# Router logits of a fused attention, MLP and expert kernel: dot products on VectorE instead of TensorE matmuls

## The chip, the cores and the metric

The program runs on one core of a Trainium2 chip. The metric is the device time of one execution in microseconds (us); each kernel is run several times. The engines of the core work in parallel, each through its own queue in order: TensorE (PE for its matmuls, PEld for its weight loads), VectorE (DVE), ScalarE (ACT), GpSimd (POOL) and SyncE (SP), which here only starts DMAs.

## The reference

Attention with a block mask over 4 batches of 576 tokens gives x (2304 tokens by 512). A dense MLP follows, and then a layer of eight experts, of which each token uses one:

```
x = attention(q, k, v)                          # [2304, 512]
h = x @ w_in                                    # [2304, 2048]
y = (max(h, 0) + alpha * min(h, 0)) @ w_out     # [2304, 512]
logits = y @ w_gate                             # [2304, 8]
e = argmax(logits); gate = softmax(logits)[e]
out = gate * (relu(y @ w1[e]) @ w2[e])
```

The change concerns the line of the logits.

## The kernel before

The 2304 tokens are cut into nine groups of 256 (g from 0 to 8, `GT` = 2 halves of 128 tokens each). A group's MLP is 16 blocks f. `l1` of a block (tile `l`, in PSUM, tag `T` with two buffers) is 12 matmuls 128x256: each product is made of three, from a high and a low part of both operands, so that the full precision is kept. VectorE applies the activation (`prelu`, tile `t`, two instructions), ScalarE makes the high part `gh`, GpSimd or VectorE the low part `gl`. `l2` of a block adds to the two accumulators `acc` (one for each half of the tokens), three matmuls 128x512 for each: two that read `gh`, then one that reads `gl`. The high and low parts of a group's input are `xh` and `xl`, four pieces of each with one buffer, made by ScalarE and VectorE out of the tile `xr`, which SP's queue loads; `xr` has one buffer.

After a group's 16th block the accumulators are copied to `y` (two tiles) and stored, and the group is routed. `turn` transposes `y` on TensorE (tile `rt`), ScalarE copies the transpose to `xt`, `logits` multiplies it with the gate's weights (tile `lg`), and VectorE copies eight columns to `L`. Then `most`, `exp` and `choose` find the expert, `rank` (two small matmuls, tile `rk`) and `place` (eleven VectorE instructions, from the sum `run` to the record `ig`) its place in the expert's list, and two scatters on GpSimd's queue (`info` out of `ig`) write it to memory. All scatters write the same tensor, so one waits until the one before it has landed.

What stands in each engine's queue, and in which order, is fixed when the program is built. Each step is a `Task` with the engine (or engines) it may run on, a cost in ns, what it reads and writes, and a priority. `order` walks through time with these costs and takes next the task that can start first, by the priority among those within 100 ns. The attention of later tokens is planned in the same list, so its blocks stand between those of the MLP in groups 0 to 5: `S` the scores, `P` the exponentials (scaled by `sm` on GpSimd or VectorE in parts), `PT` their transposes, `o` the product with v. Groups 6 to 8 have no attention left. The expert layer runs after the plan. Two costs matter here:

```
pl.add([("POOL", 780), ("DVE", 480)], lo, [t, gh], [gl], -5)
for i in range(GT):
    pl.add(("POOL", 1100), lambda on, i=i: steps.scatter(i), [("ig", g)], [("info", g, i)], pr, (1024, 1))
```

The routing of group g runs while group g+1 is computed.

Of the kernel before, what the change touches and what calls it, by code (L numbers as in the profile page):

```python
# [8 lines left out]
F32 = mybir.dt.float32  # L9
# [10 lines left out]
P = 128  # L20
# [3 lines left out]
NT, DM = B * S, H * D  # L24
FF = 2048
E, F2 = 8, 1024
GT = 2
G = P * GT
# [5 lines left out]
RATE = 300  # L34
FIRST = 12
LAG = 2
SC = 1.0 / float(D) ** 0.5
KC = 512 + P
QK = KC + S
# [183 lines left out]
def cols(n):  # L223

    return max(n / 2.4 + 12, 108)
# [67 lines left out]
class Attention:  # L293
# [24 lines left out]
    def plan(A, pl):  # L318
# [4 lines left out]
        for p, c in A.units():  # L323
            left.append(A.unit(pl, p, c, A.prio(p, c), A.soon(p, c), left))
            if (p < HP or A.soon(p, c)) and len(left) > LAG - 1:
                left.pop(0)()
# [21 lines left out]
    def early(A, pl):  # L348
# [3 lines left out]
        for p in range(2 * HP):  # L352
# [8 lines left out]
            def scale(on, p=p, i=i):  # L361
                y = pl[i][:, p % 2, 0:EARLY]
                nc.scalar.mul(y, y, SC)

# [51 lines left out]
    def unit(A, pl, p, c, pr, soon, left):  # L416
# [44 lines left out]
        fn, keys = scores1 if p < NPLAIN or soon else scores, Ss + [("step", 0)]  # L461
        if len(left) == LAG:
            left.pop(0)(ns, fn, ks, keys, pr)
# [146 lines left out]
class Mlp1:  # L610
# [6 lines left out]
    def plan(A, pl):  # L617
        for g in range(NG):
            A.tokens(pl, g)
            for f in range(16):  # L620
                A.l1(pl, g, f)
                if f:
                    A.l2(pl, g, f - 1)
            A.l2(pl, g, 15)
            if g == 0:
                A.W1.split(pl)
            if g < NG - 1:
                A.fins(pl, g)
                A.route_plan(pl, g)

    def tokens(A, pl, g):

        nc, x = A.nc, ("xr", g)
        if g == 0:
            return
        t0, t1 = g * G, g * G + G
        halves = [("xT", p, z) for p in range(NPAIR) for z, (a, b) in enumerate(Attention.HALVES) if a + p // HP * S < t1 and b + p // HP * S > t0]
        if g > 1:
            pl.buf(x, "xr", (P, 4, G))

            def load(on):
                nc.sync.dma_start(pl[x], A.xT[:, g * G:(g + 1) * G].rearrange("(k p) t -> p k t", p=P))

            pl.add(("SP", 450), load, halves, [x], -10, (524288, 180))
        for k in range(4):
            def take(k=k):
                return pl[x][:, k] if g > 1 else pl["xo", k, 1][:, 0:G]

            def hi(on, k=k, take=take):
                nc.scalar.copy(pl["xh", g, k], take())  # L650

            def lo(on, k=k, take=take):
                nc.vector.tensor_sub(pl["xl", g, k], take(), pl["xh", g, k].bitcast(F32))

            for z in ("xh", "xl"):
                pl.buf((z, g, k), f"{z}{k}", (P, G), F32R)
            x = ("xr", g) if g > 1 else ("xo", k, 1)
            pl.add(("ACT", 400), hi, [x], [("xh", g, k)], -10)
            pl.add(("DVE", 470), lo, [x, ("xh", g, k)], [("xl", g, k)], -10)

    def l1(A, pl, g, f):
        nc, l, t, gh, gl = A.nc, ("l", g, f), ("t", g, f), ("gh", g, f), ("gl", g, f)
        pl.buf(l, "T")
        c = slice(P * (f % 4), P * (f % 4) + P)
        pr = 100000 + 100 * (16 * g + f)
        keys = [("i", f // 4, k) for k in range(4)]
        ws = [n for key in keys for n in A.W1.names(key, g)]

        def prelu(on, out):
            x = pl[l][:, 0:G]  # L670
            nc.vector.tensor_scalar(pl[out], x, 0.0, A.K.al[:, f:f + 1], op0=ALU.min, op1=ALU.mult)  # L671
            nc.vector.scalar_tensor_tensor(pl[out], x, 0.0, pl[out], op0=ALU.max, op1=ALU.add)  # L672

        if g == 0:
            pl.buf(gh, "gh", (P, G))

            def plain(on):
                for k in range(4):
                    nc.tensor.matmul(pl[l][:, 0:G], lhsT=A.W1.w[keys[k]][:, c], rhs=pl["xr", g][:, k], start=k == 0, stop=k == 3)

            pl.add(("PE", 16 * cols(G)), plain, ws + [("xr", g)] + [("x0", k) for k in range(4)], [l, ("l1", g, f)], pr)
            pl.add(("DVE", 930), lambda on: prelu(on, gh), [l, ("al",)], [gh], -5)
            return

        pl.buf(t, "t", (P, G))
        pl.buf(gh, "gh", (P, G), F32R)
        pl.buf(gl, "gl", (P, G), F32R)

        def first(on):
            for k in range(4):  # L690
                (wh, wl), xh, xl = (A.W[keys[k]][:, z] for z in range(2)), pl["xh", g, k], pl["xl", g, k]
                for j, (a, b) in enumerate(((wh, xh), (wh, xl), (wl, xh))):
                    nc.tensor.matmul(pl[l][:, 0:G], lhsT=a[:, c], rhs=b, start=k == 0 and j == 0, stop=k == 3 and j == 2)  # L693

        def hi(on):
            (nc.scalar.copy if on == "ACT" else nc.vector.tensor_copy)(pl[gh], pl[t])  # L696

        def lo(on):
            (nc.gpsimd if on == "POOL" else nc.vector).tensor_sub(pl[gl], pl[t], pl[gh].bitcast(F32))  # L699

        pl.add(("PE", 12 * cols(G)), first, ws + [("l1", g - 1, 15)] + [(z, g, k) for z in ("xh", "xl") for k in range(4)], [l, ("l1", g, f)], pr)
        pl.add(("DVE", 930), lambda on: prelu(on, t), [l, ("al",)], [t], -5)
        pl.add([("ACT", 420), ("DVE", 300)], hi, [t], [gh], -5)
        pl.add([("POOL", 780), ("DVE", 480)], lo, [t, gh], [gl], -5)
# [36 lines left out]
    def route_plan(A, pl, g):  # L741
        st, pr = {}, 60000 + 100 * g
        nc = A.nc
        quick = True
        steps = A.route(g, lambda i: pl["y", g, i], st)
        if quick:
            for i in range(GT):
                ps, xt, lg = ("rt", g, i), ("xt", g, i), ("lg", g, i)
                pl.buf(ps, "T")
                pl.buf(xt, "xt")  # L750
                pl.buf(lg, "T")
                pl.add(("PE", 500), lambda on, i=i, ps=ps: steps.turn(i, pl[ps]), [("y", g, i)], [ps], 0)
                pl.add(("ACT", 600), lambda on, xt=xt, ps=ps: nc.scalar.copy(pl[xt], pl[ps]), [ps], [xt], 0)
                pl.add(("PE", 460), lambda on, i=i, xt=xt, lg=lg: steps.logits(i, pl[xt], pl[lg]), [xt], [lg], 0)
                pl.add(("DVE", 160), lambda on, i=i, lg=lg: steps.take(i, pl[lg]), [lg], [("L", g)], 0)
        else:
            for e in range(E):
                wg = ("wg", g, e)
                pl.buf(wg, "wg")
                pl.add(("SP", 450), lambda on, e=e, wg=wg: nc.sync.dma_start(pl[wg], A.wgT[e:e + 1, :].to_broadcast([P, DM])), [("wgT",)], [wg], pr, (262144, 200))  # L760
                for i in range(GT):
                    pl.add(("DVE", 760), lambda on, i=i, e=e, wg=wg: steps.dot(i, e, pl[wg]), [wg, ("y", g, i)], [("L", g)], pr)
        if quick:
            pr = 0
        pl.add(("DVE", 450), lambda on: steps.most(), [], [("L", g)], pr)
        pl.add(("ACT", 300), lambda on: steps.exp(), [("L", g)], [("ex", g)], pr)
        pl.add(("DVE", 1000), lambda on: steps.choose(), [("L", g), ("ex", g)], [("oh", g)], pr)
        rk = ("rk", g)
        pl.buf(rk, "T")
        pl.add(("PE", 300), lambda on: steps.rank(pl[rk]), [("oh", g)], [rk], 0 if quick else 50000)  # L770
        pl.add(("DVE", 2200), lambda on: steps.place(pl[rk]), [rk, ("ex", g), ("oh", g), ("run", g)], [("ig", g), ("run", g + 1)], pr)
        for i in range(GT):
            pl.add(("POOL", 1100), lambda on, i=i: steps.scatter(i), [("ig", g)], [("info", g, i)], pr, (1024, 1))
# [5 lines left out]
class Route:  # L779
# [21 lines left out]
    def take(A, i, lg):  # L801
        A.nc.vector.tensor_copy(A.L()[:, i], lg[:, 0:E])

    def dot(A, i, e, wg):
        t = A.ml.bp.tile([P, 512], F32, tag="xt", bufs=1, name=f"dot{A.n}_{i}_{e}")
        A.nc.vector.scalar_tensor_tensor(t, A.y(i), 1.0, wg, op0=ALU.mult, op1=ALU.mult, accum_out=A.L()[:, i, e:e + 1])

    def most(A):
# [482 lines left out]
                    remainder(r)  # L1291


def moe_kernel(tc, qk, v, qke, ve, w_in, w_out, alpha, w_gate, w1, w2, out):
    nc = tc.nc
    with ExitStack() as ctx:
        dp = ctx.enter_context(tc.tile_pool(name="dram", bufs=1, space=DRAM))
        xT = dp.tile([DM, NT], F32, name="xT")
        x2 = dp.tile([NT + 1, DM], F32, name="x2")
        wgT = dp.tile([E, DM], F32, name="wgT")  # L1300
        info = dp.tile([E * NT, 2], I32, name="info")
        cp = ctx.enter_context(tc.tile_pool(name="consts", bufs=1))
        wp = ctx.enter_context(tc.tile_pool(name="weights", bufs=32))
# [8 lines left out]
        pl, banks, hold = Plan(), Slots(), {}  # L1312
# [121 lines left out]
        ex.run(hold["base"], todo, od, lambda: od.all(K.run[(NG - 1) % 2][0:1, GT]))  # L1434


_INS = ['qk', 'v', 'qke', 've', 'moe_w_in', 'moe_w_out', 'moe_alpha', 'moe2_w_gate', 'moe2_w1', 'moe2_w2']
_OUTS = [((NT, DM), 'float32')]


# [46 lines left out]
```

## Time and profile before

| | |
|---|---|
| three runs | 950.98, 951.15 and 956.93 us, median 951.15 |
| the profiled execution | 951.48 us, of which the profile's span is 949.7 |
| mean granted TensorE clock | 0.976 of full speed |
| busy: PE, PEld | 892.8 and 763.4 us |
| busy: DVE, ACT, POOL | 499.5, 409.7 and 294.1 us |

Busy times add up over the whole span; which engine sets the pace is read stage by stage. Times in the rows are counted from the span's start.

### The profile page before, as it was taken

Reading aid. Unit: us, or ns where it says so; the run is one execution under the profiler, and the core shown is the slowest. Engines: PE = TensorE matmul, PEld = TensorE weight load, DVE = VectorE, ACT = ScalarE, POOL = GpSimd, SP = SyncE. Lnnn points to the kernel's source line nnn. Section 1 sums busy time; section 2 is a strip of 40 time slices with the busy share of each in tenths; the row PEclk is TensorE's granted clock in tenths of the full one; section 3 lists DMA queues with packets and bytes.
Section 4 is the critical chain, followed back from the end, with each engine's and each line's share of the span. In section 5 each row is a group of like instructions: output and inputs, shape, how many; then the busy total and the mean of one; then the engine's idle time right before and its main releaser. Section 6 shows DMA issues by size and latency. Waiting matters only on the chain. (4 is left out here: it accounts for less than half of the span.)

```text
span 949.7 us, 17897 instructions
## 1 busy us (share of the span) xinstructions
PE 892.8 (94%) x6329; PEld 763.4 (80%) x6329; DVE 499.5 (53%) x1215; ACT 409.7 (43%) x1037; POOL 294.1 (31%) x312
## 2 busy tenths in 40 slices
PE   7999989999999999999999999999889998998884
PEld 6656658888888888888999999979778987988763
DVE  4999896657546555656434353546215211613450
ACT  7777765454455446454312121223215222523451
POOL 1555673323343432443222223241212111111110
PEclk9999999999999999999999999999999998998997
DMA  8981002312302122001001010043526211622551
GB/s 340 362 317 56 23 20 74 75 48 71 75 28 76 48 59 94 28 27 36 31 2 45 1 45 2 23 123 101 170 88 222 68 47 56 198 62 80 169 163 62
DMA packets 46267, 85.80 MB, mean 90 GB/s; under 512 B 12191, under 2 KB 18991, under 8 KB 46128
## 3 DMA queue, kind: packets, MB, share of 16 engines
q1 hardware_dynamic: 35264, 64.20, 20.7%
q0 software_dynamic: 4240, 11.56, 3.8%
q10 hardware_dynamic: 6624, 8.39, 2.5%
q8 instruction: 63, 1.03, 0.5%
q14 instruction: 76, 0.62, 0.2%
HBM read 70.85 MB, written 13.67 MB: 89 GB/s over the span
## 5 line engine op out<-in xcount | busy, mean ns | idle before, releaser
L693 PE MATMUL l<-xh,wi 128*128 128x256 f32 x1024 | 206.0, 287 | 0.0
L693 PEld LDWEIGHTS l<-xh,wi 128*128 128x128 f32 x1024 | 167.0, 191 | 4.2 <-issue 0.5
L721 PE MATMUL acc<-wo,gh 128*128 128x512 f32 x512 | 167.3, 408 | 0.0
L693 PE MATMUL l<-xl,wi 128*128 128x256 f32 x512 | 145.0, 283 | 0.1
L699 POOL TENSOR_TENSOR gl<-t,gh 128x256 fp32r<-128x256 f32 x103 | 78.5, 764 | 193.3 <-ACT gh L696 158.4
L671 DVE TENSOR_SCALAR t<-l,al 128x256 f32<-128x256 f32 x128 | 61.9, 484 | 141.6 <-PE l L693 136.1
L696 ACT CAST gh<-t 128x256 fp32r<-128x256 f32 x124 | 50.4, 406 | 186.1 <-DVE t L672 105.3
L529 POOL TENSOR_SCALAR P<-P,sm 128x256 f32<-128x256 f32 (+4 forms) x66 | 78.4, 1195 | 107.7 <-ACT gh L696 39.8
L721 PE MATMUL acc<-wo,gl 128*128 128x512 f32 x256 | 101.0, 394 | 2.8 <-POOL gl L699 2.8
L693 PEld LDWEIGHTS l<-xl,wi 128*128 128x128 f32 x512 | 97.8, 191 | 4.0 <-issue 0.5
L721 PEld LDWEIGHTS acc<-wo,gh 128*128 128x128 f32 x512 | 87.0, 191 | 11.3 <-issue 0.5
L478 DVE TENSOR_REDUCE nb<-S 128x1 f32<-128x256 f32 (+4 forms) x160 | 70.1, 477 | 40.2 <-PE S L455 25.9
L523 ACT COPY F<-PT 128x384 f32<-128x384 f32 (+2 forms) x124 | 57.6, 479 | 52.8 <-PE PT L518 51.5
L495 ACT ACTIVATE P<-S,nb 128x128 f32<-128x128 f32 (+3 forms) x128 | 67.0, 531 | 14.3 <-DVE nb L478 12.9
L518 PE MATMUL PT<-ident,P 128*128 128x128 f32 (+1 forms) x400 | 64.7, 281 | 6.4 <-DVE xo L572 3.9
L518 PEld LDWEIGHTS PT<-ident,P 128*128 128x128 f32 (+1 forms) x400 | 45.9, 141 | 20.0 <-issue 3.5
L721 PEld LDWEIGHTS acc<-wo,gl 128*128 128x128 f32 x256 | 48.2, 188 | 14.7 <-POOL gl L699 3.7
L1031 PE MATMUL l<-cxh,e 128*128 128x256 f32 x320 | 58.3, 282 | 1.0 <-ACTq L1266 1.0
L1031 PE MATMUL Y<-e,hh 128*128 128x512 f32 x176 | 57.2, 406 | 0.0
L672 DVE SCALAR_TENSOR_TENSOR t<-l,t 128x256 f32<-128x256 f32 x128 | 54.3, 425 | 4.4
L988 DVE TENSOR_TENSOR e<-raw,e 128x512 fp32r<-128x512 f32 x68 | 43.9, 686 | 21.4 <-ACT e L987 17.8
L562 PE MATMUL o<-F,v 128*64 128x128 f32 (+2 forms) x832 | 53.4, 264 | 0.0
(373 smaller groups left out, 1677.8 us busy)
## 6 DMA issues: line engine op xcount, KB each, us to landing
raw<-in_moe_w_dram SPq DMA_DIRECT2D x96, 256.0 KB
qk<-in_qk_dram SPq DMA_DIRECT2D x16, 608.0 KB
rawi<-in_moe_w_in_dram SPq DMA_DIRECT2D x16, 512.0 KB
rawo<-in_moe_w_out_dram SPq DMA_DIRECT2D x16, 512.0 KB
v<-in_v_dram SPq DMA_DIRECT2D x16, 320.0 KB
x<-y ACTq DMA_DIRECT2D x16, 256.0 KB
xr<-xT SPq DMA_DIRECT2D x7, 512.0 KB
qe<-in_qke_dram SPq DMA_DIRECT2D x8, 256.0 KB
```

The costliest lines, as they stand in the source:

```text
L478: nc.vector.tensor_reduce(pl["nb", p, c][:, 2 * k + j:2 * k + j + 1], pl[Ss[j]][:, a:b], axis=AX.X, op=ALU.max, negate=True)
L495: nc.scalar.activation(pl[x][:, a:b], pl[Ss[j]][:, a:b], AF.Exp, bias=nb, scale=1.0, accum_out=pl["sm", p, c][:, 2 * k + j:2 * k + j + 1])
L518: nc.tensor.transpose(pl[t][0:w, k], pl[x][:, P * k:P * k + w], A.K.ident)
L523: f(pl[F][:, 0:n], pl[t][:, 0:n])
L529: (nc.gpsimd if on == "POOL" else nc.vector).tensor_scalar(y, y, pl["sm", p, c][:, k:k + 1], None, op0=ALU.mult)
L562: nc.tensor.matmul(y, lhsT=v[0:w, 2 * kc + h], rhs=f, start=kc == 0, stop=kc == c, skip_group_check=True)
L671: nc.vector.tensor_scalar(pl[out], x, 0.0, A.K.al[:, f:f + 1], op0=ALU.min, op1=ALU.mult)
L672: nc.vector.scalar_tensor_tensor(pl[out], x, 0.0, pl[out], op0=ALU.max, op1=ALU.add)
L693: nc.tensor.matmul(pl[l][:, 0:G], lhsT=a[:, c], rhs=b, start=k == 0 and j == 0, stop=k == 3 and j == 2)
L699: (nc.gpsimd if on == "POOL" else nc.vector).tensor_sub(pl[gl], pl[t], pl[gh].bitcast(F32))
L721: nc.tensor.matmul(pl[acc], lhsT=x[:, c], rhs=w, start=f == 0 and j == 0, stop=f == 15 and j == 2)
L1031: A.nc.tensor.matmul(ps, lhsT=x[a], rhs=w[b], start=first and q == 0, stop=last and q == 2)
```

## The change

Groups 1 to 6 (`DOTS`) are routed without `turn`, `xt`, `logits` and their `T` buffers. In their place the gate's weights, handed over transposed as `wgT` (eight rows of 512), are copied by DMA to all 128 partitions, two rows at a time, into the buffer of `xr`. For each row and each half of the tokens one VectorE instruction multiplies `y` by the row and sums along it into one column of `L`: 16 instructions a group, the products going to the tile `xt`. The first load waits for the `xl` of the group that follows, the next one for the four instructions of the one before it, and the load of `xr` two groups on waits for all of them. Groups 0, 7 and 8 are routed as before.

Block 15 of a group has a priority that puts it next to block 14, and `l1` of blocks 0 and 15 is two tasks of six matmuls, each waiting for its half of `xh` and `xl`.

```
+DOTS = (1, 2, 3, 4, 5, 6)
...
             A.tokens(pl, g)
+            if g and g - 1 in DOTS:
+                A.route_plan(pl, g - 1)
...
-            pl.add(("SP", 450), load, halves, [x], -10, (524288, 180))
+            pl.add(("SP", 450), load, halves + [("L", g - 2)] * (g - 2 in DOTS), [x], -10, (524288, 180))
...
-        pr = 100000 + 100 * (16 * g + f)
+        pr = 100000 + 100 * (16 * g + f) - (90 if f == 15 else 0)
...
-        pl.add(("PE", 12 * cols(G)), first, ws + [("l1", g - 1, 15)] + [(z, g, k) for z in ("xh", "xl") for k in range(4)], [l, ("l1", g, f)], pr)
+        for ks in ((0, 1), (2, 3)) if f in (0, 15) else (range(4),):
+            xs = [(z, g, k) for z in ("xh", "xl") for k in ks]
+            pl.add(("PE", 3 * len(ks) * cols(G)), lambda on, ks=ks: first(on, ks), ws + [("l1", g, 14) if f == 15 else ("l1", g - 1, 15)] + xs, [l, ("l1", g, f)], pr)
...
-        quick = True
+        quick = g not in DOTS
...
+            junk, got = ("xt", g), [("xl", g + 1, k) for k in range(4)]
+            pl.buf(junk, "xt")
+            for e in range(0, E, 2):
+                wg = ("xr", "wg", g, e)
+                pl.buf(wg, "xr", (P, 2, DM))
+                pl.add(("SP", 450), lambda on, e=e, wg=wg: nc.sync.dma_start(pl[wg], A.wgT[e:e + 2, :].unsqueeze(0).to_broadcast([P, 2, DM])), got, [wg], -20, (524288, 250))
+                for k in range(2):
+                    for i in range(GT):
+                        pl.add(("DVE", 690), lambda on, i=i, e=e, k=k, wg=wg: steps.dot(i, e + k, pl[wg][:, k], pl[junk]), [wg, ("y", g, i)], [junk, ("L", g)], pr)
```

As the order follows from the plan, it moves in all engines from group 1 on. Three places show how. The first is GpSimd's queue while group 6 is computed and group 5 is routed. Names carry group and block; the last number only counts tiles. Before:

```order
L699 TENSOR_TENSOR gl_6_2_6479<-t_6_2_6451,gh_6_2_6461 128x256
L846 TENSOR_SCALAR ig5_6513<-pid_90 128x2
L699 TENSOR_TENSOR gl_6_3_6537<-t_6_3_6494,gh_6_3_6522 128x256
L854 DMA info_60<-ig5_6513,si5_6508 18432x2 x2
L699 TENSOR_TENSOR gl_6_5_6591<-t_6_5_6570,gh_6_5_6576 128x256
L699 TENSOR_TENSOR gl_6_6_6617<-t_6_6_6606,gh_6_6_6609 128x256
```

And in the changed kernel:

```order
L703 TENSOR_TENSOR gl_6_13_6755<-t_6_13_6725,gh_6_13_6749 128x256
L853 TENSOR_SCALAR ig5_6792<-pid_89 128x2
L703 TENSOR_TENSOR gl_6_14_6808<-t_6_14_6771,gh_6_14_6780 128x256
L861 DMA info_59<-ig5_6792,si5_6787 18432x2 x2
L703 TENSOR_TENSOR gl_6_15_6846<-t_6_15_6819,gh_6_15_6833 128x256
L703 TENSOR_TENSOR gl_7_0_6908<-t_7_0_6873,gh_7_0_6892 128x256
```

The two scatters have moved from the group's start to its end, where `gl` of block 15 stands behind them; before, block 4's `gl` was VectorE's, and block 5's stood behind them. Group 7 has the same rows with the numbers of groups 6 and 7.

The second place is TensorE's queue from `rk` of group 5 on. Before (of a block `l` the first matmul stands here, and of the `acc` between, the first):

```order
L830 MATMUL rk_5_6497<-oh5_6485,ones_79 128x16
...
L721 MATMUL acc_6_1_6411<-wo_2_922,gh_6_2_6461 128x512 x2
...
L693 MATMUL l_6_4_6524<-xh_6_0_6318,wi_1_0_1056 128x256
...
L721 MATMUL acc_6_0_6405<-wo_3_958,gh_6_3_6522 128x512 x2
...
L693 MATMUL l_6_5_6549<-xh_6_0_6318,wi_1_0_1056 128x256
...
L721 MATMUL acc_6_0_6405<-wo_4_1205,gh_6_4_6562 128x512 x2
L721 MATMUL acc_6_0_6405<-wo_4_1205,gl_6_4_6565 128x512
...
L693 MATMUL l_6_6_6578<-xh_6_0_6318,wi_1_0_1056 128x256
```

Behind that row come `l` of block 7 and then the `acc` of block 5. In the changed kernel:

```order
L837 MATMUL rk_5_6774<-oh5_6759,ones_78 128x16
...
L727 MATMUL acc_6_0_6414<-wo_13_1564,gh_6_13_6749 128x512 x2
...
L697 MATMUL l_6_15_6801<-xh_6_0_6310,wi_3_0_1499 128x256
...
L727 MATMUL acc_6_1_6422<-wo_13_1564,gh_6_13_6749 128x512 x2
...
L727 MATMUL acc_6_0_6414<-wo_14_1587,gh_6_14_6780 128x512 x2
...
L727 MATMUL acc_6_1_6422<-wo_14_1587,gh_6_14_6780 128x512 x2
...
L697 MATMUL l_7_0_6848<-xh_7_0_6826,wi_0_0_726 128x256
...
L727 MATMUL acc_6_0_6414<-wo_15_1596,gh_6_15_6833 128x512 x2
L727 MATMUL acc_6_0_6414<-wo_15_1596,gl_6_15_6846 128x512
L697 MATMUL l_7_0_6848<-xh_7_2_6838,wi_0_2_776 128x256
```

`rk` now stands before block 15, and six of the twelve matmuls of the next group's block 0 come ahead of the `acc` of block 15, six behind its first half.

The third place is GpSimd's queue in group 4, where attention stands between the blocks (`P_13_3_1` is a part of attention's exponentials; the name of a `PT` tells the same pair and block). Before:

```order
L854 DMA info_60<-ig3_4911,si3_4906 18432x2 x2
L699 TENSOR_TENSOR gl_4_3_4975<-t_4_3_4962,gh_4_3_4967 128x256
L529 TENSOR_SCALAR P_13_3_1_5012<-P_13_3_1_5012,sm_13_3_5010 128x512
L529 TENSOR_SCALAR P_13_4_0_5086<-P_13_4_0_5086,sm_13_4_5087 128x256
L699 TENSOR_TENSOR gl_4_6_5196<-t_4_6_5166,gh_4_6_5180 128x256
```

And in the changed kernel:

```order
L861 DMA info_59<-ig3_5122,si3_5117 18432x2 x2
L530 TENSOR_SCALAR P_13_3_1_5136<-P_13_3_1_5136,sm_13_3_5134 128x512
L703 TENSOR_TENSOR gl_4_10_5224<-t_4_10_5198,gh_4_10_5213 128x256
L530 TENSOR_SCALAR P_13_4_0_5221<-P_13_4_0_5221,sm_13_4_5222 128x256
L530 TENSOR_SCALAR P_13_4_1_5241<-P_13_4_1_5241,sm_13_4_5222 128x320
```

The scatters have moved from block 3 to block 10 of the group, and the piece of `P` that was second behind them is first.

## Rows read from the trace of the kernel before

**Rows 1.** The page, busy time (share of the span) and instructions of each engine:

```profile
PE 892.8 (94%) x6329; PEld 763.4 (80%) x6329; DVE 499.5 (53%) x1215; ACT 409.7 (43%) x1037; POOL 294.1 (31%) x312
```

**Rows 2.** Windows: length; PE, PEld, DVE, ACT, POOL busy; granted clock; DMA share, GB/s:

```profile
496.90:544.90 48.00, 48.00 (x317) 43.94 (x316) 19.42 (x56) 10.05 (x24) 13.57 (x18) 1.00 0.07 23
212.40:288.10 75.70, 75.28 (x622) 65.22 (x621) 46.84 (x130) 38.35 (x113) 28.59 (x29) 1.00 0.19 55
621.40:625.00 3.60, 3.60 (x16) 3.24 (x15) 0.91 (x2) 0.42 (x3) 0.74 (x1) 0.53 0.04 1
```

**Rows 3.** Timeline in group 8: start, length, engine, instruction; in brackets the idle time before:

```profile
601.24 0.60 PE L790 MATMUL rt<-ident,y 128*128 128x128 f32 x4
601.60 0.70 PE L721 MATMUL acc<-wo,gh 128*128 128x512 f32 x2
...
603.07 0.95 PE L794 MATMUL lg<-wg,xt 128*128 128x8 f32 x8
603.88 0.63 PE L790 MATMUL rt<-ident,y 128*128 128x128 f32 x4
...
604.28 0.38 PE L693 MATMUL l<-xh,wi 128*128 128x256 f32 x1
...
605.81 0.96 PE L794 MATMUL lg<-wg,xt 128*128 128x8 f32 x8
606.62 0.70 PE L721 MATMUL acc<-wo,gh 128*128 128x512 f32 x2
...
610.24 0.29 PE L830 MATMUL rk<-oh,ones 128*128 128x16 f32 x2
...
610.60 0.71 PE L721 MATMUL acc<-wo,gh 128*128 128x512 f32 x2
```

**Rows 4.** Timeline, group 8 further on:

```profile
612.81 0.63 PE L721 MATMUL acc<-wo,gh 128*128 128x512 f32 x2
...
613.50 0.63 PE L721 MATMUL acc<-wo,gh 128*128 128x512 f32 x2
...
613.83 1.03 POOL L854 DMA_INDIRECT info<-ig,si  x1 [1.76 <-DVE t L671]
...
617.07 0.63 PE L721 MATMUL acc<-wo,gh 128*128 128x512 f32 x2
618.23 0.97 POOL L854 DMA_INDIRECT info<-ig,si  x1 [3.36 <-DMA info<-ig,si]
619.21 1.42 POOL L699 TENSOR_TENSOR gl<-t,gh 128x256 fp32r<-128x256 f32 x2
...
620.01 0.50 PE L721 MATMUL acc<-wo,gl 128*128 128x512 f32 x1 [2.31 <-POOL gl L699]
```

**Rows 5.** Timeline in group 2, attention between the blocks:

```profile
233.16 0.29 PE L830 MATMUL rk<-oh,ones 128*128 128x16 f32 x2
...
240.07 0.97 POOL L854 DMA_INDIRECT info<-ig,si  x1 [2.71 <-DMA info<-ig,si]
...
240.37 0.95 PE L562 MATMUL o<-F,v 128*64 128x64 f32 x20
...
242.00 0.73 PE L721 MATMUL acc<-wo,gh 128*128 128x512 f32 x2
...
243.48 0.77 PE L518 MATMUL PT<-ident,P 128*128 128x128 f32 x5 [0.42 <-POOL P L529]
```

**Rows 6.** Groups by line and form: count, busy us, mean ns of one, idle before:

```profile
L529 POOL TENSOR_SCALAR P<-P,sm 128x256 f32<-128x256 f32 x26 | 27.1, 1044 | 33.9 <-DVE sm L506 16.1 <-ACT gh L696 12.6 <-PE acc L721 4.8
L529 POOL TENSOR_SCALAR P<-P,sm 128x512 f32<-128x512 f32 x11 | 20.9, 1896 | 19.9 <-ACT gh L696 15.9 <-DVE sm L503 2.3 <-PE o L562 1.7
...
L406 DVE SCALAR_TENSOR_TENSOR qkl<-qk,qkh 128x640 fp32r<-128x640 f32 x10 | 8.2, 820 | 0.3
```

**Rows 7.** Timeline, SP's start of a 512 KB load of `xr`:

```profile
549.18 0.36 SPq L642 DMA_DIRECT2D xr<-xT  x1
```

**Rows 8.** Window in which that load ends, columns as in rows 2:

```profile
552.00:552.50 0.50, 0.50 (x7) 0.50 (x6) 0.00 (x0) 0.35 (x2) 0.40 (x1) 1.00 0.09 27
```

More of the change, by code (lines that the diff above doesn't have):

```diff
@@ L628, in plan @@
                 A.fins(pl, g)
-                A.route_plan(pl, g)
+                if g not in DOTS:
+                    A.route_plan(pl, g)
     def tokens(A, pl, g):
@@ L687, in l1, with first @@
         pl.buf(gl, "gl", (P, G), F32R)
-        def first(on):
-            for k in range(4):
+        def first(on, ks=range(4)):
+            for k in ks:
                 (wh, wl), xh, xl = (A.W[keys[k]][:, z] for z in range(2)), pl["xh", g, k], pl["xl", g, k]
@@ L756, in route_plan @@
         else:
[L757 to L764, printed above, removed]
+            junk, got = ("xt", g), [("xl", g + 1, k) for k in range(4)]
[7 more added lines that the diff above has]
+                        pl.add(("DVE", 690), lambda on, i=i, e=e, k=k, wg=wg: steps.dot(i, e + k, pl[wg][:, k], pl[junk]), [wg, ("y", g, i)], [junk, ("L", g)], pr)
+        pr = 0
         pl.add(("DVE", 450), lambda on: steps.most(), [], [("L", g)], pr)
@@ L769, in route_plan @@
         pl.buf(rk, "T")
-        pl.add(("PE", 300), lambda on: steps.rank(pl[rk]), [("oh", g)], [rk], 0 if quick else 50000)
+        pl.add(("PE", 300), lambda on: steps.rank(pl[rk]), [("oh", g)], [rk], 0)
         pl.add(("DVE", 2200), lambda on: steps.place(pl[rk]), [rk, ("ex", g), ("oh", g), ("run", g)], [("ig", g), ("run", g + 1)], pr)
@@ L802, in take, with dot @@
         A.nc.vector.tensor_copy(A.L()[:, i], lg[:, 0:E])
-    def dot(A, i, e, wg):
-        t = A.ml.bp.tile([P, 512], F32, tag="xt", bufs=1, name=f"dot{A.n}_{i}_{e}")
+    def dot(A, i, e, wg, t):
         A.nc.vector.scalar_tensor_tensor(t, A.y(i), 1.0, wg, op0=ALU.mult, op1=ALU.mult, accum_out=A.L()[:, i, e:e + 1])
@@ L1291, in run, with moe_kernel @@
                     remainder(r)
-def moe_kernel(tc, qk, v, qke, ve, w_in, w_out, alpha, w_gate, w1, w2, out):
+def moe_kernel(tc, qk, v, qke, ve, w_in, w_out, alpha, w_gate, wgT, w1, w2, out):
     nc = tc.nc
@@ L1299, in moe_kernel @@
         x2 = dp.tile([NT + 1, DM], F32, name="x2")
-        wgT = dp.tile([E, DM], F32, name="wgT")
         info = dp.tile([E * NT, 2], I32, name="info")
@@ L1434, in moe_kernel @@
         ex.run(hold["base"], todo, od, lambda: od.all(K.run[(NG - 1) % 2][0:1, GT]))
-_INS = ['qk', 'v', 'qke', 've', 'moe_w_in', 'moe_w_out', 'moe_alpha', 'moe2_w_gate', 'moe2_w1', 'moe2_w2']
+_INS = ['qk', 'v', 'qke', 've', 'moe_w_in', 'moe_w_out', 'moe_alpha', 'moe2_w_gate', 'wgT', 'moe2_w1', 'moe2_w2']
 _OUTS = [((NT, DM), 'float32')]
@@ L1472 @@
     inputs = {**inputs, **_laid_out(_np, *(_np.asarray(inputs[x]) for x in "qkv"))}
+    inputs["wgT"] = _np.asarray(inputs["moe2_w_gate"]).T
     for name in _INS:
```

## The prediction

> **What bounds the kernel now.** I read the page's engine line first: TensorE is busy for 94% of the span, VectorE for 53%, GpSimd for 31% [rows 1]. A mean hides stages, so the windows come next. In one whole group without attention, 6 (496.9 to 544.9 us), TensorE is busy for 48.00 of 48.00 us and VectorE for 19.42; in group 2, with attention between the blocks, it is 75.28 of 75.70 and 46.84 [rows 2]. So in the groups that the change touches TensorE is the limit, any work taken from it shortens the span, and VectorE has room: 28.6 us in the one, 28.9 in the other. What interrupts TensorE is found in the timeline, where its idle time stands in brackets: 2.31 us in group 8, 0.42 in group 2, both for an instruction of GpSimd that stands behind the two scatters of a route [rows 4, 5]. These waits are the heart of this forecast, because the change moves the scatters, and the plan reckons only 1.1 us for each.
>
> **Taken away: the logits on TensorE.** The timeline of group 8 has the routing of group 7, done as all are done before. From the first transposes (601.24) to the end of the second half's logits (606.62) are 5.38 us [rows 3]. In between stand two halves of an `l2` (each two matmuls 128x512, 0.69 from one start to the next [rows 4]) and one `l` (604.28 to 605.81, 1.53 with its edge [rows 3]; I take 1.44, three of them following each other at that pace). The routing's share is 5.38 - 1.38 - 1.44 = 2.56, with edges 2.6 us. Six groups give 15.6. In group 2 the stall of 0.42 before `PT` [rows 5] goes with its old neighbours: **16.0 us** in all. ScalarE's copies of the transposes and VectorE's takes of the eight columns go too, but neither engine was waited for.
>
> **Added: the dot products.** The nearest row is a VectorE instruction of the same kind on 128x640, 820 ns [rows 6]; for 512 elements 0.66 us by proportion. It has no sum along the row, so that I bound one from below by 0.66 and from above by 0.86 (0.2 more, my allowance for reading out the sum). Sixteen are 10.5 to 13.8 us a group, against the 28 us and more that VectorE has free [rows 2]: **0** in the sum. What could make it cost is their order: a dot in front of a `prelu` delays the block's `gh`, and `l2` runs behind `l1` by two blocks. Clusters of four dots (2.6 to 3.4 us) fit in that lag.
>
> **Added: the loads.** Six groups have four loads of 512 KB, which copy two rows of the weights to all partitions. The nearest row is the load of `xr`, also 512 KB: started at 549.18, still moving in the window that begins at 552.0, where the DMA share is down to 0.09 [rows 7, 8]; so about 2.9 us. Three of a group's four loads wait for the four dots of the one before. SP's queue is in order, so attention's loads of q, k and v stand behind that wait; they are ahead of their use by a buffer. On VectorE two `prelu`s and their parts stand between the last dot of a pair of rows and the first of the next, about 4.2 us at TensorE's pace of one block (1.44 + 2 x 1.38 = 4.2, since VectorE keeps step with it). 2.9 is less than 4.2: **0**, and a rival below if it isn't.
>
> **Moved: block 15 ahead, and blocks 0 and 15 in halves.** Before, TensorE has no idle time over a whole group, its boundary included [rows 2]. There is nothing to save: **0**. The halves cost no further matmul.
>
> **Moved: the scatters.** This is the term that decides. The route now ends later in the group, and what stands behind its scatters on GpSimd changes. A route's second scatter waits until the first has landed, and GpSimd's queue stands still meanwhile. In group 8 `rk` starts at 610.24 and the second scatter ends at 619.20: 9.0 us, of which 1.76 and 3.36 are waits of GpSimd [rows 3, 4]. In group 2 it is 233.16 to 241.04: 7.9 [rows 5]. I take 8.4, the middle. The next `gl` behind them costs 0.7 to start and end its first part, or TensorE gets it at 620.01 when GpSimd became free at 619.21 [rows 4]: **8.4 + 0.8 = 9.2 us after `rk`**. A part of `P` that stands first is there after 8.4 + 1.0 = 9.4 (128x256) or 8.4 + 1.9 = 10.3 (128x512) [rows 6], a 128x512 behind a `gl` after 11.0.
>
> TensorE's arrival at the matmul that needs it follows from the queue (order of the changed kernel) and these lengths: `rk` 0.36 [rows 3], `l` 1.44, half an `l2` 0.69, `o` with `S` 1.63 (240.37 to 242.00) [rows 5], `PT` 0.4 a block (estimate from its 0.77 for five transposes [rows 5]). By group and the route in it:
>
> - group 2: `rk`, `o` and `S`, `l`, `l2`, `l`: 0.36 + 1.63 + 1.44 + 1.38 + 1.44 = 6.25, then `PT` wants a `P` of 9.4: 3.2 us of stall.
> - group 3: arrival 8.5 against a `gl` at 9.2, 0.7; then a `PT` that had followed at 9.4 against a `P` at 11.0, 1.6: together 2.3.
> - group 4: arrival 7.35 against the `P` 128x512 that is now first, 10.3: 2.95.
> - group 5: the `gl` is wanted at 10.7, after 9.2: 0.
> - group 6: half `l2` 0.69, `l` 1.44, three halves 2.07, half an `l` 0.72, and the two `gh` matmuls 0.46 that stand ahead of `gl` of block 15: with `rk` 5.74, against 9.2: 3.45.
> - group 7: the same with one half `l2` more, 6.46 against 9.2: 2.7.
> - group 8: as before [rows 4], no difference.
>
> The sum is **14.6 us**. [...] I count it behind the four stalls of over 2.4 us and not behind the pieces in group 3: 4 x 1.7 = **6.8**.
>
> **The sum.** 14.6 + 6.8 - 16.0 = +5.4. The profiled execution took 951.48 (span 949.7), 0.3 over the median of 951.15, nothing that matters here. **951.15 + 5.4 = 956.5 us.** A measurement of this kernel tells some 1% from no change, 9.5 us: faster is below 941.6, slower above 960.7.
>
> **The rivals.**
>
> A. *The scatters hide.* GpSimd's lateness is not felt where the true order in time differs from the plan, for instance because the route runs earlier or TensorE arrives later than I add up. For it: in group 2 the stall was only 0.42 [rows 5] although an equal scatter pair stood there. If the stalls with attention (groups 2 to 4: 8.45, with 2 x 1.7 clock) don't come, 956.5 - 11.9 = 944.7; if none comes, 951.15 - 16.0 = 935.1. Against it: group 8 shows the same row of scatters and `gl` stalling by 2.31 [rows 4] with an arrival of 7.3 after `rk`, later than those that I count on. Chances 0.12 and 0.10.
>
> B. *The weights' loads come late (slower).* All partitions read the same 4 KB, and no row shows such a load. Its place: SP's queue between two sets of four dots. It decides from 4.2 us; each us more delays VectorE, and behind it the blocks' `gh`, by up to three waits in six groups, 18 us. At 5.2 us a load: 956.5 + 18 = 974.5. Against it: the data moved are those of `xr`, 2.9 us [rows 7, 8]. Chance 0.12.
>
> C. *The dots run at half the rate*, about 2 x 0.66 = 1.3 us, and clusters of four take 5.2 us, more than the 4.2 in which TensorE uses up its lag. Sixteen are 21 us; 19.4 + 21 = 40 of about 45 us in group 6 [rows 2] would still fit by the sum, but each of four clusters would hold up `gh` by about a us: 6 x 4 x 0.8 = 19 us, 975. Row against it: two fp32 operands in SBUF took 820 ns for 640 [rows 6], 1.28 ns an element, the overhead included; but that instruction has no sum. Chance 0.07.
> [...]
>
> D. *VectorE is late for `most`, `choose` and `place`*, since these stand behind the dots, or TensorE waits at `rk`, which is in its queue at a place that the plan reckoned with 0.69 for a dot. At 0.86 a dot the chain of sixteen is 2.7 us later; if half of it is felt as waits in six groups, that is 8 us: 964 (961 to 970). Against it: between dots stand `prelu`s whose pace TensorE sets, so the chain has slack of its own. Chance 0.09.
>
> That the change doesn't do what it says is excluded by the order: the transposes and logits of groups 1 to 6 are gone from TensorE's queue.
>
> **How the numbers follow.** The forecast case has 0.50: 948 to 962, where the low end has the scatters a us faster everywhere (five groups lose 5 us) and two stalls too short to bring the clock down (3.4), and the high end the 9.0 us of group 8's route everywhere and the clock falling behind the two pieces of group 3 as well. Rivals A 0.22, B 0.12, C 0.07, D 0.09. The range holds what is left when the lowest tenth (no stall at all) and the worst of B and C are cut off: 941 to 974. Faster by over 1%: A's second case and a little of its first, 0.12. Slower by over 1%: B, C, most of D, and a sixth of the forecast case, 0.34. Within 1%: 0.54.
>
> **What the changed profile would show.** For the gain: no `rt` and `lg` rows between groups 2 and 7, and a whole group's period shorter by 2.6 us where no stall is. For the scatters: TensorE's idle time put down to GpSimd's `gl` (groups 6 and 7, 2.5 to 3.5 us) and `P` (groups 2 to 4), each just behind a pair of scatters, and the granted clock near 0.5 after it. For B: VectorE waiting for the DMA of the weights; for C: a mean over 1 us at the dots' line; for D: idle time at `rk` put down to VectorE. The forecast is wrong if TensorE's queue meets the scatters elsewhere than I place them: a stall more or less is 4 to 5 us with its clock.

## The result and the profile after

The changed kernel takes 956.2 us (median of 20 runs, 950.2 to 963.5) against 951.8 for the kernel before (20 runs, 946.2 to 956.9): ratio 1.0057, 95% interval 1.0035 to 1.0079. The forecast was 956.5 us, 0.6% slower. The profiled execution has a span of 952.4 us against 949.7.

The engine line of the changed kernel's page, to be held against [rows 1]:

```profile
PE 880.6 (92%) x6185; PEld 750.1 (79%) x6185; DVE 560.2 (59%) x1387; ACT 402.2 (42%) x1022; POOL 310.6 (33%) x323
```

TensorE has 144 matmuls and 12.2 us less, VectorE 60.7 us more, and the span is longer. Where it went shows in one window that holds the same work in both: from the same `acc` matmul of group 0 to the end of the last `acc` of the MLP. First the kernel before, then the changed one (columns as in rows 2):

```profile
121.81:651.76 529.95, 526.19 (x3948) 458.29 (x3949) 294.28 (x812) 222.70 (x619) 187.76 (x203) 0.99 0.16 48
```

```profile
121.68:654.94 533.26, 515.94 (x3804) 447.02 (x3805) 354.82 (x984) 215.05 (x604) 203.89 (x214) 0.98 0.23 71
```

Length less busy time is TensorE's idle time: 3.8 us before, 17.3 after. The busy time holds also what half clock adds (stretches granted 0.50). I take that as 1 less the granted clock, summed over windows of 1 us: 3.4 us before, 10.2 after (0.5 of these fall into the waits themselves and are counted twice, so that the work after is up to 0.5 higher than what follows). What is left is TensorE's work at full clock: 526.2 - 3.4 = 522.8 before, 515.9 - 10.2 = 505.7 after. So **the change took 17.1 us of work from TensorE, and gave back 13.5 us of waiting and 6.8 us of half clock**: +3.2, and the window is 3.3 us longer. The half clock in it is an estimate, some tenth too high: in the changed kernel three matmuls 128x512 took 1.28 us from start to start at 0.50 (552.19 to 553.47) and 0.70 at 1.00 (557.62 to 558.32), 1.8 times as long rather than twice, so that the 6.8 and the 17.1 may each be 0.6 too high.

Nearly all the waits are behind the scatters. In group 6 of the changed kernel, where the kernel before has none [rows 2], GpSimd's timeline reads:

```profile
543.41 1.04 POOL L861 DMA_INDIRECT info<-ig,si  x1 [2.04 <-DVE ig L858]
548.54 0.96 POOL L861 DMA_INDIRECT info<-ig,si  x1 [4.09 <-DMA info<-ig,si]
549.53 0.73 POOL L703 TENSOR_TENSOR gl<-t,gh 128x256 fp32r<-128x256 f32 x1
```

The second scatter waits 4.09 us for the first to land, and `gl` of block 15 starts as soon as it is out. TensorE's timeline has `rk` of that route, and the waits of groups 2, 4, 6, 7 and 8:

```profile
276.22 0.48 PE L519 MATMUL PT<-ident,P 128*128 128x128 f32 x2 [2.46 <-POOL P L530]
...
413.22 1.12 PE L519 MATMUL PT<-ident,P 128*128 128x128 f32 x4 [3.18 <-POOL P L530]
...
540.22 0.29 PE L837 MATMUL rk<-oh,ones 128*128 128x16 f32 x2
...
550.32 0.80 PE L727 MATMUL acc<-wo,gl 128*128 128x512 f32 x1 [4.06 <-POOL gl L703]
...
602.12 0.50 PE L727 MATMUL acc<-wo,gl 128*128 128x512 f32 x1 [2.61 <-POOL gl L703]
...
623.23 0.50 PE L727 MATMUL acc<-wo,gl 128*128 128x512 f32 x1 [2.19 <-POOL gl L703]
```

In group 6 TensorE arrives at 550.32 - 4.06 = 546.26, 6.0 us after `rk`, and gets `gl` 10.1 us after it. In group 3 one wait of 0.86 for a `P` stands behind the scatters; another of 0.21, at 339.19, comes ahead of that route's `rk` (341.76) and has nothing to do with them. Group 5 has none. One wait is of another kind, in group 1, which is the first with its blocks in the new form and whose routing (of group 0) is as before:

```profile
142.78 0.39 PE L697 MATMUL l<-xh,wi 128*128 128x256 f32 x1 [1.75 <-DVE t L676]
```

The granted clock behind the five waits of over 2 us (windows):

```profile
276.00:280.00 4.00, 3.78 (x13) 3.12 (x14) 0.76 (x3) 1.53 (x4) 3.11 (x4) 0.57 0.00 0
413.00:417.00 4.00, 3.78 (x17) 3.50 (x18) 0.32 (x2) 1.11 (x3) 1.82 (x4) 0.57 0.00 2
549.00:557.00 8.00, 6.68 (x29) 6.30 (x30) 1.53 (x4) 1.48 (x3) 1.97 (x3) 0.57 0.33 117
602.00:606.00 4.00, 3.88 (x25) 3.53 (x26) 0.91 (x2) 2.20 (x5) 0.80 (x2) 1.00 0.35 131
624.00:628.00 4.00, 4.00 (x18) 3.63 (x17) 1.06 (x3) 0.56 (x2) 0.73 (x1) 0.58 0.09 19
```

A mean of 0.57 over 4 us loses 1.7 us, over 8 us 3.4. Behind the wait of 4.06 the stretch is twice as long as behind the others, and behind that of 2.61 there is none.

The dots and their loads, as the view of the tile `xr_wg` sums them up (duration in ns: least, median, most):

```profile
L813 DVE SCALAR_TENSOR_TENSOR xt<-y,xr_wg x96: 660/683/1279, 221.0 to 588.3; 128x512 f32<-128x512 f32 x96
L813 DVE DVE_READ_ACCUMULATOR xt<-y,xr_wg x96: 75/82/85, 221.8 to 588.9; 128x1 f32 x96
...
  DMA xr_wg<-in_wgT_dram: 5.1, 3
```

A dot is 683 ns and 82 ns more for reading out the sum. VectorE waited for the weights three times, 5.1 us in all; the load issued at 526.62 let the next dot start at 530.45, 3.8 us.

### The profile page after: what moved, and what is told of

The parts are those of the page before. It is cut to its first block, busy times and chain, and to the rows that moved or that the text cites. A ratio compares the mean times of both kernels' runs of the same rounds, so it can differ in the third digit from the quotient of the medians.

```text
span 952.4 us, 17816 instructions
## 1 busy us (share of the span) xinstructions
PE 880.6 (92%) x6185; PEld 750.1 (79%) x6185; DVE 560.2 (59%) x1387; ACT 402.2 (42%) x1022; POOL 310.6 (33%) x323
## 5 line engine op out<-in xcount | busy, mean ns | idle before, releaser
L697 PE MATMUL l<-xh,wi 128*128 128x256 f32 x1024 | 208.6, 288 | 1.7 <-DVE t L676 1.7
L697 PEld LDWEIGHTS l<-xh,wi 128*128 128x128 f32 x1024 | 169.5, 193 | 6.6 <-DVE t L676 2.2
L703 POOL TENSOR_TENSOR gl<-t,gh 128x256 fp32r<-128x256 f32 x107 | 81.5, 762 | 183.3 <-ACT gh L700 150.7
L530 POOL TENSOR_SCALAR P<-P,sm 128x256 f32<-128x256 f32 (+4 forms) x71 | 89.0, 1260 | 101.9 <-ACT gh L700 46.2
L813 DVE SCALAR_TENSOR_TENSOR xt<-y,xr_wg 128x512 f32<-128x512 f32 x96 | 73.7, 768 | 8.9 <-DMA xr_wg<-in_wgT_dram 5.1
L519 PE MATMUL PT<-ident,P 128*128 128x128 f32 (+1 forms) x400 | 65.7, 284 | 12.2 <-POOL P L530 6.7
L727 PEld LDWEIGHTS acc<-wo,gl 128*128 128x128 f32 x256 | 48.9, 191 | 21.2 <-POOL gl L703 10.2
```

What stands on the lines that cost most here:

```text
L519: nc.tensor.transpose(pl[t][0:w, k], pl[x][:, P * k:P * k + w], A.K.ident)
L530: (nc.gpsimd if on == "POOL" else nc.vector).tensor_scalar(y, y, pl["sm", p, c][:, k:k + 1], None, op0=ALU.mult)
L727: nc.tensor.matmul(pl[acc], lhsT=x[:, c], rhs=w, start=f == 0 and j == 0, stop=f == 15 and j == 2)
```

## The experiments

**Theory**: the logits' removal is worth what it was reckoned at; what eats it is GpSimd's queue, which stands behind the pair of scatters because the second waits for the landing of the first, and which the plan doesn't know of. **Rivals**: VectorE is late with the dots; the new order as such is worse; the block ahead and the halves are what costs.

The measure for all is the same window as above. Work is TensorE's busy time less what half clock adds; "ratio" is to the kernel before on the same chip, with its 95% interval. The experiments ran on three chips, on which the kernel before has medians of 948.3 us (1 to 4), 951.3 (5 to 8) and 948.3 (9 and 10), so that kernels are compared by the ratio.

| kernel | window | idle | half clock | work | us, median | ratio |
|---|---|---|---|---|---|---|
| before | 530.0 | 3.8 | 3.4 | 522.8 | 951.8 | 1 |
| changed | 533.3 | 17.3 | 10.2 | 505.7 | 956.2 | 1.0057 (1.0035 to 1.0079) |
| 1: second scatters left out | 512.5 | 4.4 | 1.7 | 506.3 | 934.1 | 0.9850 (0.9805 to 0.9895) |
| 2: scatters paced | 515.7 | 2.6 | 7.8 | 505.2 | 933.8 | 0.9821 (0.9767 to 0.9874) |
| 3: dots alone | 530.5 | 14.4 | 8.5 | 507.5 | 949.9 | 0.9998 (0.9968 to 1.0028) |
| 4: dots of 64 columns | 529.5 | 16.1 | 6.8 | 506.6 | 946.0 | 0.9981 (0.9949 to 1.0013) |
| 5: before, paced | 525.1 | 0.8 | 1.7 | 522.7 | 947.1 | 0.9952 (0.9925 to 0.9980) |
| 6: block 15 and halves alone | 542.0 | 15.9 | 3.4 | 522.6 | 966.0 | 1.0166 (1.0135 to 1.0198) |
| 7: paced, groups 0 to 7 by dots | 506.5 | 3.6 | 1.4 | 501.5 | 947.3 | 0.9957 (0.9934 to 0.9981) |
| 8: paced, dots alone | 512.1 | 1.8 | 1.7 | 508.6 | 935.6 | 0.9838 (0.9811 to 0.9865) |
| 9: paced, groups 0 to 6 by dots | 510.5 | 3.4 | 2.7 | 504.4 | 932.6 | 0.9828 (0.9775 to 0.9880) |
| 10: as 9, without block 15 and halves | 511.8 | 3.5 | 1.7 | 506.6 | 935.4 | 0.9869 (0.9817 to 0.9921) |

Window, idle, half clock and work are of the profiled execution of each; the runs of one kernel lie some 1% apart (the changed one's 20 from 950.2 to 963.5 us), and those with a lower mean granted clock are mostly the longer ones (of these 20, the ten shorter have 0.975 in the mean, the ten longer 0.970), so that a single window's half clock isn't that of the median.

**1. The second scatter of groups 1 to 6 left out.**

```
-... lambda on, i=i: steps.scatter(i) ...
+... lambda on, i=i: None if i and g in DOTS else steps.scatter(i) ...
```

The prefill of the lists is changed to go with it.

> The changed kernel with one thing left out: the second scatter of the routes of groups 1 to 6 is not issued, so that half of these tokens is missing from the experts' lists and other, distinct rows of those same tokens stand in the lists' unused places. The order of everything else is the same. Theory (the gain is eaten by GpSimd's queue standing behind the pair of scatters): GpSimd is free some 4.3 us earlier in each of these routes (the 3.36 us of waiting and 0.97 us of the second scatter), earlier than TensorE arrives, so the stalls of groups 2 to 7 (2.46, 0.21, 0.86, 3.18, 4.06, 2.61: 13.4 us) and the three stretches at half clock behind them (1.7 us each, 3.4 in group 6 with its longer one: 6.8 us) go: the expert layer begins at about 654.8 - 20 = 635 us instead of 654.8, the whole takes about 936 us. Rival (the stalls come from VectorE being late with the dots, or from the new order as such): the expert layer begins at 650 or later and the whole takes 951 us or more.

The expert layer began at 636.6 us. All waits for GpSimd in groups 2 to 7 were gone but the one of 0.21 that stands ahead of its scatters, and with them the half clock behind; in group 8, where both scatters still stand, TensorE still waited:

```profile
606.56 0.50 PE L727 MATMUL acc<-wo,gl 128*128 128x512 f32 x1 [2.04 <-POOL gl L703]
```

Its window (columns as in rows 2):

```profile
124.25:636.74 512.49, 508.04 (x3804) 440.88 (x3805) 356.05 (x984) 214.94 (x604) 198.41 (x208) 1.00 0.24 74
```

With the same queues in the same order, the second scatter alone accounts for 12.9 us of idle time and 6.8 of half clock; another 1.7 of half clock is missing in group 8, where the wait of 2.04 had none behind it this time. The theory holds, and the rivals that blame VectorE or the order as such fall.

**2. The whole kernel with scatters that the plan sees land.**

```
-... [("ig", g)], [("info", g, i)], pr, (1024, 1))
+... [("ig", g)], [("info", g, i), ("info",)], pr, (1024, 1))
```

> The changed kernel complete, with one key more in the plan: both scatters write a common key, so that the plan lets the second one start only when it reckons the first to have landed (1.1 + 1.0 + 2.0 us after its start), and puts other work of GpSimd between them. Theory: the stalls behind the scatters shrink below 1 us each, in group 8 too (2.19 us and 1.7 of clock there): expert layer from about 654.8 - 13.4 - 6.8 - 3 = 632 us, the whole about 934 us (930 to 942). Rival (order, not the blocked queue): stalls of the same sum appear elsewhere, 950 us or more.

Ratio 0.9821, 933.8 us. In group 6 the plan now puts `gl` of block 15 between the two scatters; GpSimd's timeline:

```profile
539.72 1.04 POOL L861 DMA_INDIRECT info<-ig,si  x1 [2.04 <-DVE ig L858]
541.01 0.77 POOL L703 TENSOR_TENSOR gl<-t,gh 128x256 fp32r<-128x256 f32 x1 [0.25 <-DVE gh L700]
543.63 0.98 POOL L861 DMA_INDIRECT info<-ig,si  x1 [1.86 <-DMA info<-ig,si]
```

No wait of TensorE behind a scatter is over 0.34 us. The window (columns as in rows 2):

```profile
122.17:637.83 515.66, 513.01 (x3803) 446.13 (x3803) 358.33 (x980) 212.83 (x601) 205.45 (x219) 0.98 0.24 74
```

The expert layer began at 637.7, later than the 632 expected, because in this execution the wait of 1.78 us in group 1, which has nothing to do with the scatters, was followed by a long stretch at half clock:

```profile
144.00:155.00 11.00, 10.74 (x53) 10.03 (x54) 4.96 (x13) 3.36 (x13) 4.71 (x5) 0.53 0.04 13
```

**3. The dots alone**, without block 15 ahead and without halves: `pr` and the loop over `ks` as in the kernel before.

> The changed kernel without the block 15 ahead and without the halves of blocks 0 and 15: the dot products alone. Theory (that part is worth nothing by itself): with TensorE's idle time and the time at half clock taken off, the MLP ends within 2 us of the changed kernel's; the scatters again stand in front of other work, so that stalls of 8 to 16 us remain, 950 to 960 us. Rival (the block ahead is what costs, or what pays): 940 us, or 965 and more.

949.9 us, at the lower edge of what was expected, and no different from the kernel before (0.9998). The scatters stand in front of other work here too (waits of 0.76, 1.96, 3.50, 2.76 and 2.29 us in groups 2, 3, 6, 7 and 8), and the sum is somewhat less. The wait of 1.75 in group 1 isn't there; two others are, of 0.78 and 1.07 for `P` at 138 to 140 us, with a stretch at half clock behind them. The work is 507.5, 1.8 us more than in the changed kernel, just inside what was expected.

**4. Dots over 64 columns.**

```
-... scalar_tensor_tensor(t, A.y(i), 1.0, wg, op0=...)
+... scalar_tensor_tensor(t[:, 0:64], A.y(i)[:, 0:64], 1.0, wg[:, 0:64], op0=...)
```

> The changed kernel with each dot product over the first 64 of 512 columns only (so other logits and other experts); loads, order and number of instructions are the same. Theory (VectorE's dots are beside the path): the stalls behind the scatters stay within 0.7 us of the changed kernel's, and the expert layer begins within 2 us of 654.8. Rival (dots are felt, by their duration of 768 ns or by the route being late): the expert layer begins 5 us earlier or more.

VectorE has 50.7 us less to do over the span (509.5 against 560.2), and TensorE waits at the same places: 2.16, 1.05, 3.07, 4.16, 1.89 and 2.03 us in groups 2, 3, 4, 6, 7 and 8; five of the six are within 0.4 us of the changed kernel's, group 7's is 0.7 less. The expert layer began at 653.1, 1.6 us earlier; the window is 3.8 us shorter, of which 3.4 are half clock. The dots are beside the path. That the whole is 10 us shorter is the expert layer's doing, which has other tokens for each expert (289 us from its begin to the end against 298), so the ratio says nothing here.

**5. The kernel before, with the common key** (the edit of experiment 2).

> The kernel before with the plan's common key for the scatters, and nothing else of the change. Theory: only the stalls that the kernel before has behind its scatters can go (0.42, 0.47 and 2.31 us, and 1.7 us of half clock): about 5 us, ratio to the kernel before 0.995 (0.991 to 0.999). Rival (the key is a better order whatever the logits cost, and most of the gain of the paced kernel is its own): 0.985 or less.

0.9952. Its waits behind the scatters are gone, 4.2 us in the median. The key alone isn't the gain of experiment 2. By the medians of 5 and 8, which ran on one chip, the dots are worth another 1.2% once the order is paced.

**6. Block 15 ahead and the halves, no dots.**

```
-DOTS = (1, 2, 3, 4, 5, 6)
+DOTS = ()
```

> The changed kernel with no group routed by dot products: what is left is block 15 ahead and blocks 0 and 15 in halves. Theory (worth nothing by itself): from the same matmul in group 0 to the end of the MLP, TensorE's busy time less what half clock adds is 522.8 us as before, within 1 us, and the ratio to the kernel before is within 0.996 to 1.004 but for stalls of the scatters, which move little. Rival (this part has a share of the gain of 17 us in TensorE's work): 521 us or less, and a ratio of 0.995 or less.

Half of this was wrong. The work is 522.6 us, as expected: the part saves nothing. But the kernel is 1.7% slower, as the order that it brings puts the scatters in front of a `gl` that is wanted soon, and the wait of 1.58 us in group 1 is there again. TensorE waits 3.25, 0.60, 2.42, 2.58 and 3.06 us for `gl` in groups 2, 3, 4, 5 and 8; in the kernel before its waits for GpSimd there were 0.42 (for a `P`), 0.47, 0, 0 and 2.31. Its window:

```profile
121.87:663.86 541.99, 526.06 (x3947) 458.05 (x3947) 296.34 (x814) 218.37 (x611) 191.24 (x210) 0.99 0.16 47
```

In group 2 GpSimd's timeline reads:

```profile
235.63 1.05 POOL L861 DMA_INDIRECT info<-ig,si  x1 [0.79 <-DVE t L675]
241.45 0.96 POOL L861 DMA_INDIRECT info<-ig,si  x1 [4.77 <-DMA info<-ig,si]
242.43 1.41 POOL L703 TENSOR_TENSOR gl<-t,gh 128x256 fp32r<-128x256 f32 x2
```

So the trap isn't the dots': any change of the order can fall into it. The expectation took the kernel before's places of the scatters for granted, without a look at the queue.

**7. Paced, with groups 0 and 7 by dots too** (`DOTS` from 0 to 7).

> The paced kernel with groups 0 and 7 routed by dot products too. Theory (each group's logits cost TensorE 2.6 to 2.9 us and nothing else waits for the route): 5 to 6 us less than the paced kernel, ratio to the kernel before 0.976. Rival (the last route is wanted by the expert layer, and a route that is later by some 20 us makes its first fetch wait): 0.982 or more, with TensorE waiting for the fetched rows longer than the 2.5 us of the changed kernel.

The rival came. The MLP is 4 us of work shorter and ends at 629.6, but the expert layer can't begin; TensorE's timeline:

```profile
645.19 1.12 PE L1011 MATMUL Tx<-ident,xg 128*128 128x128 f32 x4 [15.60 <-DMA xg<-x,it]
```

The last route but one is wanted by the first expert's fetch. There the latency of the dots counts, which is hidden everywhere else; with group 7 back on TensorE (experiment 9) the wait is gone.

**8. Paced, dots alone** (the edits of 2 and 3).

> The paced kernel without block 15 ahead and without the halves. Theory: within 0.4% of the paced kernel, ratio 0.980 to 0.986, no stall over 1 us behind a pair of scatters. Rival (the block ahead is what lets the paced order work): stalls of several us at the ends of groups, 0.988 or more.

0.9838, with no wait over 0.3 us. The block ahead isn't needed for the gain. The window:

```profile
121.77:633.83 512.06, 510.27 (x3803) 440.63 (x3803) 354.36 (x974) 216.30 (x608) 214.60 (x218) 1.00 0.25 74
```

**9. Paced, groups 0 to 6 by dots.**

> The paced kernel with group 0 routed by dot products too, group 7 on TensorE as in the changed kernel. Theory (the kernel with groups 0 and 7 lost at the first expert's fetch alone, 15.6 us, and its MLP had 4 us less of TensorE work than the paced kernel's, half of it from group 0): no wait of over 3 us for the fetched rows, 2 us less than the paced kernel, ratio to the kernel before 0.980 (0.975 to 0.984). Rival (group 0's dots come while VectorE still makes the weights and are felt): stalls on VectorE in group 1, 0.985 or more.

932.6 us, ratio 0.9828; the first wait for fetched rows over 1 us is one of 2.63 in the expert layer (2.50 in the changed kernel). The work is 0.8 us less than in experiment 2. Whether it is faster than that one can't be told from these runs.

**10. The same without block 15 ahead and halves.**

> The same without block 15 ahead and without the halves. Theory (that part is worth nothing once the scatters don't block): within 0.4% of the kernel with it, 0.977 to 0.986. Rival (it pays once the scatters are out of the way): slower than it by 0.5% or more.

0.9869, 0.3% above its twin in the median and with an interval that overlaps; a wait of 1.02 us for `P` at 290.7 is new. Neither theory nor rival is shown.

The versions that beat both kernels are the paced ones: 2 and 9 take some 933 us, 1.7 to 1.8% less than the kernel before and, by the two ratios, 2.3% less than the changed one.

## Why the prediction was right, point by point

- **What bounds the kernel.** TensorE, and its waits for GpSimd behind the scatters: right. Experiment 1 takes one scatter of each pair away and the expert layer begins 18 us earlier.
- **The logits, 15.6 us.** The work fell by 17.1 us, with the dots alone by 15.3 (experiment 3) and 14.2 (experiment 8): right in size for the sum, with an error of a us or two. From one `rk` to the next in groups without attention it is less than the 2.6 reckoned: 48.17 us before (562.07 to 610.24), 46.07 in experiment 2 (536.53 to 582.60), 2.1 us.
- **The dots, 0.** Right: 683 + 82 ns, within the 0.66 to 0.86 us given (of the 0.2 allowed for reading out the sum, 0.08 came), and experiment 4 leaves the waits where they were. Rival D has nothing for it, and rival A neither: waits came in all the groups named. (The case that the prediction held against A is misread: TensorE arrived at that `gl` 620.01 - 2.31 - 610.24 = 7.46 us after `rk`, not 7.3, and one arrival that it counts on, 8.5 in group 3, is later still.)
- **The dots at half rate (rival C).** The median of 683 ns for 512 elements stands beside the 820 for 640 [rows 6] at nearly the same pace (1.33 and 1.28 ns an element); that row has two sources in SBUF as well. A third row of the changed kernel has one of its sources in PSUM and no sum (the expert layer's `hl<-l,hh`, 128x512): a median of 692 ns. So there is no halving against either, and what the sum costs is the 82 ns of its own row.
- **The loads, 0 (rival B).** Nearly right: 3.3 to 3.8 us from issue to use, in the three cases where VectorE waited for a load, rather than 2.9; still under the 4.2 from which it decides. These waits are 5.1 us in all, and TensorE waited for none of them.
- **Block 15 and halves, 0.** Mis-sized. No work is saved without the dots (experiment 6), and with them 1.8 to 3.4 us (experiment 3 against the changed kernel, 8 against 2, 10 against 9), for which I have no cause that the runs show. Against it stands the wait of 1.75 us in group 1 for `t`, which is there in all the kernels with this part (1.07 to 1.78) and in none without. In the paced kernels the window less its half clock is 2.3 to 2.5 us shorter with the part (9 against 10, 2 against 8), too little for the medians to tell. And the part moves the scatters as much as the dots do: without pacing the kernel takes 0.9998 of the kernel before with the dots alone, 1.0057 with both and 1.0166 with this part alone. The slowdown that was forecast hangs on it as much as on the dots, which a term of 0 doesn't tell.
- **The scatters, 14.6 us.** Right, with small errors. Predicted and measured for groups 2 to 7: 3.2 and 2.46; 2.3 and 0.86; 2.95 and 3.18; 0 and 0; 3.45 and 4.06; 2.7 and 2.61. The sum is 13.2. Of the two pieces in group 3 only that for `P` came; the `gl` was there when TensorE reached it. GpSimd was free 7.7 to 9.3 us after `rk` (8.4 taken). In groups 2, 4, 6 and 7 TensorE arrived 0.2 to 0.5 us later than added up (6.7, 7.8, 6.0 and 6.7 against 6.25, 7.35, 5.74 and 6.46).
- **Half clock, 6.8 us.** The sum is right and the way to it wrong, so that the agreement is luck: four stretches of 1.7 were forecast (3.6 us at 0.53, the window from 621.40 in [rows 2], lose 3.6 x 0.47 = 1.7), and there were three, one of them of double length, while group 7's wait had none behind it. Nor do the other runs bear out that it comes behind each wait of over 2.4 us: none came behind 3.06 (experiment 6) and 2.76 (experiment 3).
- **The sum, +5.4.** Between the medians it is +4.4, by the ratio's interval 3.3 to 7.5. That the forecast time and the median differ by 0.3 us is luck as well: the terms are off by one or two us each, in both directions, and the kernel before has a median of 951.8 over 20 runs rather than the 951.15 of three.

## What to carry to other kernels

Taking work from the engine that is the limit pays only as long as the other queues still deliver on time: when a planner sets the order, look in the new order for the instruction that blocks its queue for longer than its modelled cost, and for who stands behind it. Here one key more in the plan, which tells it that a scatter blocks the next one until it has landed, turned +0.6% into -1.8%, and was worth 0.5% where nothing had been moved. Work that is moved to an engine with room costs latency instead of throughput: here it was free where the result is wanted much later, and cost 15.6 us where the next stage waited for it.

## What the runs showed of the hardware

- The wait for the landing of a scatter isn't a fixed time: where the second of a pair stood right behind the first, GpSimd waited from 2.5 to 4.8 us before it (2.52 and 4.09 in the changed kernel, 4.77 in experiment 6).
- Eighteen of the 96 dots took 0.89 to 1.28 us rather than 0.68, and each of the eighteen overlapped an instruction of GpSimd; of the 78 others 22 did by 0.1 us or more, so that overlap alone doesn't decide. With fifteen of them a `gl` had started 0.01 to 0.42 us before the dot, as in this pair of the changed kernel, the first row of GpSimd's timeline and the second of VectorE's:

```profile
533.56 0.73 POOL L703 TENSOR_TENSOR gl<-t,gh 128x256 fp32r<-128x256 f32 x1 [3.44 <-ACT gh L700]
```

```profile
533.60 1.24 DVE L813 SCALAR_TENSOR_TENSOR xt<-y,xr_wg 128x512 f32<-128x512 f32 x1
```

  The four dots that had begun 0.07 to 0.35 us ahead of a `gl` (258.93, 365.52, 478.57 and 503.74) took 0.67 to 0.69, and these `gl` 0.95 to 1.19 rather than the 0.74 of the median. The eighteen are 8 us longer in all than at the median, beside the path.
- A wait of TensorE of 2 to 4 us is mostly but not always followed by half clock (granted 0.50 in the windows of 1 us inside the stretches of the kernel before and the changed one). In the windows of the kernel before, the changed one and experiments 1, 3, 4 and 6 TensorE waits twenty times for 1.89 to 4.16 us for GpSimd. Behind thirteen of these waits there is half clock, behind 1.89 us (experiment 4) as behind 4.16; behind seven there is none, 3.06 us (experiment 6) the longest. Its length isn't given by the wait's either: behind the 4.06 us of the changed kernel it lost 3.4 us, behind the 4.16 of experiment 4 only 1.7, and behind a wait of 1.78 us for VectorE in experiment 2 it lost 5.1. Which waits bring the clock down stays open.
